# Tables loaded through ScalarE's queue, attention spread over the gated MLP, output stores issued by ScalarE

## The chip, the cores and the metric

One core of one Trainium2 chip runs the whole program. The metric is the device time of one execution in microseconds (us). Engines are named as in the profile: PE is TensorE (PEld its weight loads), DVE is VectorE, ACT is ScalarE, POOL is GpSimd, SP is SyncE, which in the kernel before only issues DMAs. Each engine runs its own instructions strictly in the order in which they were written.

## The reference, cut to what matters

```python
B, H, S, D = 4, 8, 768, 64                      # attention with a decaying state, 8 heads
for t in range(S):
    state = gamma * state + outer(k[:, :, t], v[:, :, t])
    y[:, :, t] = scale * einsum('bhd,bhde->bhe', q[:, :, t], state)
x = y.transpose(0, 2, 1, 3).reshape(B, S, H * D)    # 4 x 768 x 512
gate_pre[s] = sum over 5 taps of conv_w[k] * x[s - 4 + k]   # causal, per channel
gate = 1 / (1 + exp(-gate_pre))
out = (gate * (x @ w_val)) @ w_out                  # two 512x512 matrices
```

## The kernel before, in words

The 768 tokens are cut in 6 chunks of 128 and the 4 batch entries are taken in turn, so attention has 24 steps `g` of (batch, chunk). A step loads 1 MB (`att`: q, k, v and k again in the layouts that the matmuls want), scales v by the decay on POOL (`decay`), multiplies q and k on PE (`scores`, into PSUM `sy`), masks the result on DVE (`mask`, into `u`), and adds on PE the part from the scores (`y_scores`), the update of the running state (`state`, in PSUM `z_ps`) and the part from the state (`y_state`, which reads copies `snap` that ACT makes). DVE then multiplies the sum by a table and writes it into `x` (`evac`). These matmuls are 64x64 in f32; each runs as two passes, so a step of a middle chunk is 128 weight loads and 128 matmuls in the profile: 32 for `scores`, 32 for `y_scores`, 16 for each of two `state`s, 32 for `y_state`.

The gated MLP works on six groups `n` of 512 rows (one chunk of all four batch entries), in four tiles `m` of 128 channels. `val_tile` is 12 matmuls of 128x512 (high and low parts of `x` against high and low parts of `w_val`), `out_tile` 12 more against `w_out`; 24 tiles of each, 576 matmuls. The gate of a tile is a convolution of five taps: the first on ACT, the others on DVE (a few on PE, `pe_tap`), then a sigmoid on ACT. `split`, `gated`, `round_gv` and `rest_gv` make the high and low parts on ACT, DVE and POOL. `store` copies an output tile out of PSUM on ACT; `send` issues its DMA on SP's queue. The two weight matrices and the taps arrive as 64-bit floats; `convert` turns each of eight weight pieces into f32 with five DVE instructions, and some on ACT and POOL.

The order of all engines comes from a planner. Every instruction is a `Step` with a due time, an engine, a cost and what it reads and writes; `plan` orders steps by due time and lets the engine that is free first take the ready step that is earliest due. Due times come from constants: the first six attention steps (`EARLY`) start at `EARLY_AT` and follow each other by `EARLY_STEP`; the other eighteen start at `LATE_AT` and follow by `LATE_STEP`; the MLP tiles start at `MLP_AT` and follow by `MLP_STEP`; `W_AT` holds the due times of the weight conversions. The costs and due times only order the instructions; nothing waits for a clock.

In the first six steps two PSUM tiles for `sy` are in use; the first `val_tile` needs the place of one of them, so it comes after all of them. From the seventh step on the scores of the next step are issued behind `y_state` of this one, in the same `sy`, which is why `y_scores` of a step waits for `evac` of the step before.

Five `att` buffers (`LB`) and four weight buffers (`WB`) set when loads can start. The DMAs of both queues share eight completion semaphores in turn, so a DMA waits for the eighth DMA before it.

In the change and the prediction "the sixth x" is the `evac` of g = 5, "the eleventh x" that of g = 10.

Of the kernel before, what the change touches and what calls it, by code (L numbers as in the profile page):

```python
# [16 lines left out]
P = 128  # L17
# [23 lines left out]
class Step:  # L41
    def __init__(self, due, engine, cost, reads, writes, fn, args):
        self.due, self.engine, self.cost, self.fn, self.args = due, engine, cost, fn, args
        self.reads, self.writes = reads, writes
        self.waits, self.then = set(), []
        self.next = []
        self.after = []
        self.ready = 0.0
        self.words = 0
        self.other = None  # L50


def plan(steps):

    steps = sorted(steps, key=lambda s: s.due)
    writer, readers, rings, users = {}, {}, {}, {}
    for i, s in enumerate(steps):
        s.index = i
        for k in s.writes:
            if isinstance(k, Slot) and k not in users:  # L60
# [24 lines left out]
    for ring in rings.values():  # L85
        for i, (k, s) in enumerate(ring):
            if i >= k.bufs:
                for b in users[ring[i - k.bufs][0]]:
                    wait(s, b)
            if i and s not in ring[i - 1][1].next:  # L90
                s.waits.add(ring[i - 1][1].index)
                ring[i - 1][1].next.append(s)
    clock, free = {}, {}

    def offer(s):
        free.setdefault(s.engine, []).append(s)
        if s.other:
            free.setdefault(s.other[0], []).append(s)

    for s in steps:  # L100
        clock.setdefault(s.engine, 0.0)
        if not s.waits:
            offer(s)
    order, words, paged = [], PAGE - 28, [0.0, 0.0]
    while any(free.values()):
        start, _, e = min(
            (max(clock[e], min(s.ready for s in f)), e, e) for e, f in free.items() if f
        )
        s = min((s for s in free[e] if s.ready <= start), key=lambda s: (s.engine != e, s.index))
        free[s.engine].remove(s)  # L110
        if s.other:
            free[s.other[0]].remove(s)
            if s.engine != e:
                s.engine, s.cost, s.fn = s.other
        order.append(s)
        clock[e] = start + s.cost
        if e == "PE" and s.words:

            left, now = s.words, start
            while left >= words:  # L120
                now += s.cost * words / s.words
                left -= words
                paged.append(now)
                now, words = max(now, paged[-2] + FETCH), PAGE
            words -= left
            clock[e] = max(clock[e], now + s.cost * left / s.words)
        for t in s.next:
            t.ready = max(t.ready, start)
            if t not in s.then:
                t.waits.discard(s.index)  # L130
                if not t.waits:
                    offer(t)
        for t in s.then:
            late = LANDING if e == "DMA" else 0.0 if t.engine == e else LATENCY
            t.ready = max(t.ready, clock[e] + late)
# [8 lines left out]
def tile_retention_gated_mlp(  # L144
# [34 lines left out]
    nc = tc.nc  # L179
# [19 lines left out]
    small_sb = const.tile([P, small.shape[1]], F32, name="small_sb")  # L199
# [20 lines left out]
    def at(due, engine, cost, reads, writes, fn, *args):  # L220
        steps.append(Step(due, engine, cost, list(reads), list(writes), fn, args))
# [12 lines left out]
        nc.sync.dma_start(out=tiles[g][:, part], in_=att[i, :, part])  # L234

    def get(dst, src):
        nc.sync.dma_start(out=dst, in_=src)

    def halves(g, what):

# [267 lines left out]
        outs[n, b, cs.start] = o_sb[:, 0:step]  # L508

    def send(n, b, cs=slice(0, DM)):  # L510
        nc.sync.dma_start(out=out[b, n * P:(n + 1) * P, cs], in_=outs.pop((n, b, cs.start)))


    warm = nc.const_aps.tensor(0.0, (P, 1), F32).bitcast(BF16)[:, 0:1]
# [15 lines left out]


    MM = 0.232
    EARLY_AT = 2.6
    EARLY_STEP = 2.8
    LATE_AT = 28.7
    LATE_STEP = 3.05
    MLP_AT = 31.2
    MLP_STEP = 10.2
    SPLIT_LEAD = 5.4
    CONV_LEAD = 6.1  # L540
    W_AT = (9.3, 15.6, 15.6, 22.7, 32.7, 35.7, 38.7, 41.7)

    loaded = {}

    def load_at(due, g):
        loaded[g] = due
        a = [("att", g % LB, "qk"), ("att", g % LB, "vk")]
        if g == 0:
            at(due, "DMA", 1.4, [], a[0:1], load, g, slice(0, 2))
            at(due, "DMA", 0.2, [], ["small"], get, small_sb, small)  # L550
            at(due, "DMA", 1.4, [], a[1:2], load, g, slice(2, 4))
            at(due, "DMA", 0.1, [], ["cwraw"], get, cw_raw,
               conv_w.bitcast(I32).rearrange("p (n two) -> p n two", two=2))
# [12 lines left out]
        if ahead and g + 1 < NG:  # L566
            scores(g + 1)

    scored, summed = {}, {}

    def attention(g, t, ahead):

# [33 lines left out]
        if b == 0:  # L606
            xbufs[c] = Slot("x", XB)
            last = [xbufs[c - 1]] + [("x", c - 1, i) for i in range(B)] if c else []
            at(t + 3.5, "ACT" if c else "DVE", 0.25, last,
               [xbufs[c]] + [("x", c, i) for i in range(B)], new_x, c)  # L610
        at(t + 5.0, "DVE", 0.62, [y, ("dec", c % 2), xbufs[c]], [("x", c, b)], evac, g)
        if g + LB < NG:
            load_at(t + 3.4, g + LB)
# [83 lines left out]
    at(0, "ACT", 1.5, [], ["table"], first_sigmoid)  # L697
    load_at(0, 0)
    for due, w, n in ((0.1, 1, 0), (0.2, 0, 1), (0.3, 1, 1), (0.4, 0, 2), (0.5, 1, 2), (0.6, 0, 3), (0.7, 1, 3), (0.8, 0, 4)):
        if w or n < LB:  # L700
            (load_w_at if w else load_at)(due, n)
        if due == 0.3:
            at(due, "DMA", 0.2, [], ["eye"], get, eye_sb, eye)
    at(5.05, "PE", 1.0, ["pos", ("att", 0, "vk")], ["sy1"], first_pos)
    at(5.06, "ACT", 0.6, ["sy1"], ["base", ("dec", 0)], base_copy)
    convert(4.0, "cw")
# [16 lines left out]
    order += [(out_tile, NU - 1, m) for m in range(NPAIR)]  # L723
    for p, (what, n, m) in enumerate(order):
        t = MLP_AT + MLP_STEP * p
# [99 lines left out]
```

## Time and profile before

| | |
|---|---|
| median of three runs | 234.3 us (234.22 to 234.41) |
| the profiled execution's own time | 235.24 us |
| its span, first to last instruction | 233.5 us |
| busy PE, DVE, ACT, POOL | 209.3, 140.2, 105.7, 105.7 us |
| mean granted PE clock | 0.954 |

The span is what the views of the profile cover; 1.74 us of the profiled execution lie outside it. The profiled execution took 0.94 us more than the median of the other runs. "Idle before, <-" names what an engine waited for; "issue" is time in which it waited for nothing that the profile shows. A busy PE is one with a matmul in flight, not PE at its peak.

### The profile page before, as it was taken

What the parts mean: (1) busy time and instruction counts of PE and PEld (TensorE: products, weight loads), DVE (VectorE), ACT (ScalarE), POOL (GpSimd) and SP (SyncE); (2) the same over time, 40 slices, a digit from 0 to 9 for tenths busy, and PEclk for the clock granted to TensorE, in tenths of its full rate; (3) what the DMA queues carried; (4) which work ended last, traced back from release to release, by engine and by line L of the source; (5) the groups of instructions that cost most, each with busy time, mean ns of one, the idle gap of its engine ahead of it and who ended that gap; (6) DMA issues with size and microseconds to landing.
All of it is one profiled execution on the core that took longest, in us unless ns stands there. A gap on an engine that the chain in (4) does not pass through costs nothing.

```text
span 233.5 us, 7952 instructions
## 1 busy us (share of the span) xinstructions
PE 209.3 (90%) x3549; PEld 163.5 (70%) x3549; DVE 140.2 (60%) x213; ACT 105.7 (45%) x218; POOL 105.7 (45%) x93
## 2 busy tenths in 40 slices
PE   8276666998799998897998999999999999999994
PEld 3166655766577776675776778888888888888884
DVE  0488678999999998322296636169617861921100
ACT  2363285238855842243544322664376426521322
POOL 0257879677996281116822020582078208220400
PEclk9975697999999999998899999999999999999999
DMA  5999979963565665545250101111111111111122
GB/s 155 381 428 413 380 276 345 414 234 117 181 219 206 243 239 199 206 173 215 65 213 3 48 4 49 45 46 45 48 45 45 45 47 63 59 58 45 45 93 90
DMA packets 8822, 36.32 MB, mean 156 GB/s; under 512 B 1106, under 2 KB 1618, under 8 KB 5844
## 3 DMA queue, kind: packets, MB, share of 16 engines
q1 hardware_dynamic: 8788, 35.82, 41.0%
q8 instruction: 28, 0.46, 0.8%
q14 instruction: 6, 0.05, 0.1%
HBM read 29.52 MB, written 6.29 MB: 153 GB/s over the span
## 4 chain that ended last, share of the span: by engine, by line
PE 61%; DVE 19%; issue 7%; POOL 5%; ACT 3%; DMA 3%; SPq 0%; POOLq 0%; ACTq 0%; DVEq 0%
PE mm L497 27%; PE mm L469 22%; DVE acc L443 9%; PE sy L297 6%; PE sy L259 3%; DMA att<-in_att_dram 3%; PE z_ps L281 3%; DVE x L342 3%; DVE u L269 2%; POOL rest L411 2%; POOL att L249 2%; DVE gate L478 1%; ACT xh L351 1%; DVE rest L415 1%; POOL wvl L430 1%
## 5 line engine op out<-in xcount | busy, mean ns | idle before, releaser
L443 DVE SCALAR_TENSOR_TENSOR acc<-x,cw_sb,acc 128x512 f32<-128x512 f32 x95 | 70.5, 753 | 17.2 <-ACT acc L441 15.1
L489 POOL TENSOR_TENSOR gvl<-gate,gvh 128x512 fp32r<-128x512 f32 x24 | 30.8, 1291 | 44.6 <-ACT gvh L485 34.4
L355 POOL TENSOR_TENSOR xl<-x,xh 128x512 fp32r<-128x512 f32 x24 | 30.5, 1284 | 31.8 <-PE mm L469 28.5
L497 PE MATMUL mm<-woh,gvh 128*128 128x512 f32 (+1 forms) x100 | 39.4, 394 | 0.0
L497 PE MATMUL mm<-wol,gvh 128*128 128x512 f32 (+1 forms) x100 | 39.3, 393 | 0.0
L497 PE MATMUL mm<-woh,gvl 128*128 128x512 f32 (+1 forms) x100 | 39.3, 393 | 0.0
L249 POOL TENSOR_TENSOR att<-att,small_sb 128x512 f32<-128x512 f32 x24 | 25.1, 1044 | 29.1 <-DMA att<-in_att_dram 27.3
L507 ACT COPY o_sb<-mm 128x512 f32<-128x512 f32 (+1 forms) x25 | 14.3, 571 | 37.0 <-PE mm L497 36.9
L269 DVE TENSOR_TENSOR u<-sy,small_sb 128x512 f32<-128x512 f32 x24 | 16.5, 686 | 24.0 <-PE sy L259 24.0
L478 DVE TENSOR_TENSOR gate<-mm,gate 128x512 f32<-128x512 f32 x24 | 16.4, 685 | 22.2 <-PE mm L469 22.2
L469 PE MATMUL mm<-xl,wvh 128*128 128x512 f32 x96 | 28.5, 407 | 0.0
L469 PE MATMUL mm<-xh,wvh 128*128 128x512 f32 x96 | 28.2, 410 | 0.0
L469 PE MATMUL mm<-xh,wvl 128*128 128x512 f32 x96 | 28.1, 404 | 0.0
L485 ACT CAST gvh<-gate 128x512 fp32r<-128x512 f32 x24 | 14.9, 620 | 26.2 <-DVE gate L478 17.6
L297 PEld LDWEIGHTS sy<-u,att 64*64 64x64 f32 x768 | 16.0, 152 | 14.4 <-issue 5.8
L259 PE MATMUL sy<-att 64*64 64x64 f32 x768 | 18.8, 232 | 7.4 <-issue 6.3
L297 PE MATMUL sy<-u,att 64*64 64x64 f32 x768 | 19.1, 243 | 5.9 <-DVE x L342 3.6
L281 PE MATMUL z_ps<-att 64*64 64x64 f32 x704 | 22.1, 240 | 2.3 <-issue 1.0
L292 ACT COPY snap<-z_ps 128x256 f32<-128x256 f32 x44 | 14.5, 371 | 19.0 <-PE z_ps L281 19.0
L281 PEld LDWEIGHTS z_ps<-att 64*64 64x64 f32 x704 | 17.3, 150 | 8.1 <-ACT snap L292 5.2
L259 PEld LDWEIGHTS sy<-att 64*64 64x64 f32 x768 | 15.9, 147 | 9.0 <-issue 7.0
L497 PEld LDWEIGHTS mm<-woh,gvh 128*128 128x128 f32 x100 | 18.9, 189 | 4.2
(46 smaller groups left out, 264.6 us busy)
## 6 DMA issues: line engine op xcount, KB each, us to landing
att<-in_att_dram SPq DMA_DIRECT2D x23, 1024.0 KB, 5.8
out_dram<-o_sb SPq DMA_DIRECT2D x23, 256.0 KB, 2.0
wst<-in_w_dram SPq DMA_DIRECT2D x8, 512.0 KB, 7.2
att<-in_att_dram SPq DMA_DIRECT2D x2, 512.0 KB, 5.5
out_dram<-o_sb SPq DMA_DIRECT2D x2, 128.0 KB, 1.7
small_sb<-in_small_dram SPq DMA_DIRECT2D x1, 68.0 KB, 4.1
eye_sb<-in_eye_dram SPq DMA_DIRECT2D x1, 64.0 KB, 8.5
cw_raw<-in_conv_w_dram SPq DMA_DIRECT2D x1, 20.0 KB, 6.4
```

Of the source, the lines that this page charges most:

```text
L249: nc.gpsimd.tensor_tensor(v, v, vd_sb[:, c, :].unsqueeze(2).broadcast_to([P, 8, HALF]), op=ALU.mult)
L259: nc.tensor.matmul(sy[cols, x, (2 * j + s) * HALF:(2 * j + s + 1) * HALF], lhsT=kT[rows, x, j, s, :], rhs=q[rows, x, j, s, :], start=True, ...
L269: nc.vector.tensor_tensor(us[g], sy[:, :, 0:256].rearrange("p x (a t) -> p x a t", t=HALF), tri_sb.unsqueeze(1).unsqueeze(1).broadcast_to( ...
L281: nc.tensor.matmul(z_ps[cols, x, b, j], lhsT=k[rows, x, j, s, :], rhs=v[rows, x, j, s, :], start=g == 0 and s == 0 and j == 0, stop=True, ...
L297: nc.tensor.matmul(sy_of(g)[cols, h, off:off + HALF], lhsT=lhsT, rhs=rhs, start=start, stop=True, skip_group_check=True,)
L355: nc.gpsimd.tensor_tensor(xl[n, ct], xs[n][:, ct, :, HALO:], xh[n, ct].bitcast(F32), op=ALU.subtract)
L443: nc.vector.scalar_tensor_tensor(acc, x[:, :, k:k + P], cw_sb[:, m, k:k + 1], acc, op0=ALU.mult, op1=ALU.add,)
L469: nc.tensor.matmul(vps[n, m], lhsT=w[:, m, ct * P:(ct + 1) * P], rhs=xx[n, ct].rearrange("p b t -> p (b t)"), start=(i == 0), stop=(i == 3 ...
L478: nc.vector.tensor_tensor(gv, vps.pop((n, m)), gv, op=ALU.mult)
L485: nc.scalar.copy(gvs[n, m][0], gate[n, m])
L489: nc.gpsimd.tensor_tensor(gvl, gate.pop((n, m)), gvh.bitcast(F32), op=ALU.subtract)
L497: nc.tensor.matmul(ops[n, b, cs.start][:, 0:cs.stop - cs.start], lhsT=gg[:, b * P:(b + 1) * P], rhs=w[:, ct, cs], start=(i == 0), stop=(i ...
```

## The change

It does five things.

1. `small`, `pos`, `conv_w` and `eye` are loaded through ACT's queue, ahead of ACT's first instruction, and the two halves of the first `att` follow each other on SP's queue. `first_pos` no longer waits for the second half of `att`.
2. On DVE the first mask is moved ahead of most of the conversion of the taps.
3. `send` issues the output DMA on ACT, a few instructions behind the copy that it sends, instead of on SP.
4. The due times change: late attention steps follow each other by 6.0 instead of 3.05, MLP tiles by 3.6 instead of 10.2, and a `val_tile` is due no earlier than its `x` is whole.
5. The planner's own cost of a fetch of PE instructions changes.

```diff
-PAGE, FETCH = 128, 4.0
+PAGE, FETCH, CROWDED = 128, 3.4, 5.0
...
     def get(dst, src):
-        nc.sync.dma_start(out=dst, in_=src)
+        nc.scalar.dma_start(out=dst, in_=src)
...
     def send(n, b, cs=slice(0, DM)):
-        nc.sync.dma_start(out=out[b, n * P:(n + 1) * P, cs], in_=outs.pop((n, b, cs.start)))
+        nc.scalar.dma_start(out=out[b, n * P:(n + 1) * P, cs], in_=outs.pop((n, b, cs.start)))
...
-    LATE_STEP = 3.05
+    LATE_STEP = 6.0
...
-    MLP_STEP = 10.2
+    MLP_STEP = 3.6
...
         if g == 0:
-            at(due, "DMA", 1.4, [], a[0:1], load, g, slice(0, 2))
-            at(due, "DMA", 0.2, [], ["small"], get, small_sb, small)
-            at(due, "DMA", 1.4, [], a[1:2], load, g, slice(2, 4))
-            at(due, "DMA", 0.1, [], ["cwraw"], get, cw_raw,
+            at(due, "DMA", 3.2, [], a[0:1], load, g, slice(0, 2))
+            at(due, "DMA", 1.6, [], a[1:2], load, g, slice(2, 4))
+            at(due, "ACT", 0.4, [], ["small"], get, small_sb, small)
+            at(due, "ACT", 0.4, [], ["pos"], get, pos_sb, pos)
+            at(due, "ACT", 0.4, [], ["cwraw"], get, cw_raw,
...
-            at(due, "DMA", 0.1, [], ["pos"], get, pos_sb, pos)
+            at(due, "ACT", 0.4, [], ["eye"], get, eye_sb, eye)
...
-            at(t0 + 12 * MM / cols + 0.2, "DMA", 0.1, [o], [], send, n, b, cs)
+            at(t0 + 12 * MM / cols + 0.2, "ACT", 0.07, [o], [], send, n, b, cs)
...
+        if what is val_tile:
+            t = max(t, whole[n] + max(SPLIT_LEAD, CONV_LEAD))
```

What this does to the order is shown at three places. The first is DVE at the start of the program; `cw_raw` is the raw taps, `wst` a raw weight piece, `sy` and `u` the scores and the masked scores. Before:

```order
L386 TENSOR_SCALAR acc<-cw_raw 128x20
L392 SCALAR_TENSOR_TENSOR top<-cw_raw,acc 128x20
L398 TENSOR_SCALAR acc<-top 128x20
L402 SCALAR_TENSOR_TENSOR rest<-cw_raw,acc 128x20
L415 SCALAR_TENSOR_TENSOR cw_sb<-acc,rest 128x20
L386 TENSOR_SCALAR acc<-wst 128x512
L269 TENSOR_TENSOR u<-sy,small_sb 128x512
```

Now, on the same engine from the same place:

```order
L388 TENSOR_SCALAR acc<-cw_raw 128x20
L394 SCALAR_TENSOR_TENSOR top<-cw_raw,acc 128x20
L271 TENSOR_TENSOR u<-sy,small_sb 128x512
L400 TENSOR_SCALAR acc<-top 128x20
L404 SCALAR_TENSOR_TENSOR rest<-cw_raw,acc 128x20
L388 TENSOR_SCALAR acc<-wst 128x512
L394 SCALAR_TENSOR_TENSOR top<-wst,acc 128x512
```

The mask of the first step stands behind two small instructions of the conversion instead of six.

The second place is PE from the first `val_tile` (g = 6) to `y_scores` of g = 7; `mm` is a tile of the MLP, `sy<-u,att` is `y_scores`, `sy<-att,snap` is `y_state`, `sy<-att` is `scores`. Before:

```order
L469 MATMUL mm<-xh,wvh 128x512 x4
L281 MATMUL z_ps<-att 64x64 x8
L297 MATMUL sy<-att,snap 64x64 x16
L259 MATMUL sy<-att 64x64 x16
L469 MATMUL mm<-xh,wvl 128x512 x4
L469 MATMUL mm<-xl,wvh 128x512 x4
L469 MATMUL mm<-xh,wvh 128x512 x2
L297 MATMUL sy<-u,att 64x64 x16
```

Now:

```order
L471 MATMUL mm<-xh,wvh 128x512 x4
L471 MATMUL mm<-xh,wvl 128x512
L283 MATMUL z_ps<-att 64x64 x8
L299 MATMUL sy<-att,snap 64x64 x16
L261 MATMUL sy<-att 64x64 x16
L471 MATMUL mm<-xh,wvl 128x512 x3
L471 MATMUL mm<-xl,wvh 128x512 x4
L471 MATMUL mm<-xh,wvh 128x512 x4
L471 MATMUL mm<-xh,wvl 128x512 x4
L471 MATMUL mm<-xl,wvh 128x512 x2
L299 MATMUL sy<-u,att 64x64 x16
```

The step holds 22 matmuls of the MLP instead of 14.

The third place is the middle of the program, SP's queue before, where stores stand between loads:

```order
L234 DMA att<-in_att_dram 128x2048 x6
L511 DMA out_dram<-o_sb 128x512
L234 DMA att<-in_att_dram 128x2048 x2
L511 DMA out_dram<-o_sb 128x512
L234 DMA att<-in_att_dram 128x2048 x2
L511 DMA out_dram<-o_sb 128x512
```

and ACT now, where the first two stores stand among copies of the state, taps and sigmoids:

```order
L294 COPY snap<-z_ps 128x256 x2
L509 COPY o_sb<-mm 128x512
L461 ACTIVATE gate<-acc 128x512
L513 DMA out_dram<-o_sb 128x512
L443 ACTIVATE acc<-x,cw_sb 128x512
L461 ACTIVATE gate<-acc 128x512
L487 CAST gvh<-gate 128x512
L509 COPY o_sb<-mm 128x512
L513 DMA out_dram<-o_sb 128x512
```

SP's queue now ends in loads alone, thirteen of them in a row; all 25 stores stand on ACT.

More of the change, by code (lines that the diff above doesn't have):

```diff
@@ L47, in __init__ @@
         self.after = []
+        self.lag = 0.0
         self.ready = 0.0
@@ L123, in plan @@
                 paged.append(now)
-                now, words = max(now, paged[-2] + FETCH), PAGE
+                slow = clock.get("DMA", 0.0) > now
+                now, words = max(now, paged[-2] + (CROWDED if slow else FETCH)), PAGE
             words -= left
@@ L134, in plan @@
             late = LANDING if e == "DMA" else 0.0 if t.engine == e else LATENCY
-            t.ready = max(t.ready, clock[e] + late)
+            t.ready = max(t.ready, clock[e] + late + s.lag)
             t.waits.discard(s.index)
@@ L532, in tile_retention_gated_mlp @@
     MM = 0.232
-    EARLY_AT = 2.6
-    EARLY_STEP = 2.8
-    LATE_AT = 28.7
-    LATE_STEP = 3.05
-    MLP_AT = 31.2
-    MLP_STEP = 10.2
-    SPLIT_LEAD = 5.4
-    CONV_LEAD = 6.1
-    W_AT = (9.3, 15.6, 15.6, 22.7, 32.7, 35.7, 38.7, 41.7)
+    EARLY_AT = 3.46
+    EARLY_STEP = 2.26
+    LATE_AT = 29.71
+    LATE_STEP = 6.0
+    MLP_AT = 31.96
+    MLP_STEP = 3.6
+    SPLIT_LEAD = 5.44
+    CONV_LEAD = 6.16
+    W_AT = (9.3, 13.0, 15.6, 22.7, 36.8, 32.1, 37.6, 38.1)
     loaded = {}
@@ L548, in load_at @@
         if g == 0:
-            at(due, "DMA", 1.4, [], a[0:1], load, g, slice(0, 2))
-            at(due, "DMA", 0.2, [], ["small"], get, small_sb, small)
-            at(due, "DMA", 1.4, [], a[1:2], load, g, slice(2, 4))
-            at(due, "DMA", 0.1, [], ["cwraw"], get, cw_raw,
+            at(due, "DMA", 3.2, [], a[0:1], load, g, slice(0, 2))
[3 more added lines that the diff above has]
+            at(due, "ACT", 0.4, [], ["cwraw"], get, cw_raw,
                conv_w.bitcast(I32).rearrange("p (n two) -> p n two", two=2))
-            at(due, "DMA", 0.1, [], ["pos"], get, pos_sb, pos)
+            at(due, "ACT", 0.4, [], ["eye"], get, eye_sb, eye)
+            for s in steps[-4:]:
+                s.lag = 5.0
         else:
@@ L567, in block_b @@
             scores(g + 1)
-    scored, summed = {}, {}
+    scored, summed, whole = {}, {}, {}
     def attention(g, t, ahead):
@@ L610, in attention @@
                [xbufs[c]] + [("x", c, i) for i in range(B)], new_x, c)
+        whole[c] = t + 5.1
         at(t + 5.0, "DVE", 0.62, [y, ("dec", c % 2), xbufs[c]], [("x", c, b)], evac, g)
@@ L692, in out_tile @@
             at(t0 + 12 * MM / cols + 0.1, "ACT", 0.6 / cols, [bank], [o], store, n, b, cs)
-            at(t0 + 12 * MM / cols + 0.2, "DMA", 0.1, [o], [], send, n, b, cs)
+            at(t0 + 12 * MM / cols + 0.2, "ACT", 0.07, [o], [], send, n, b, cs)
     for i in range(WARM):
         at(0, "PE", 0.43, [], [Slot("acc", 2) if i < 2 else "sy1"], warm_up, i)
-    at(0, "ACT", 1.5, [], ["table"], first_sigmoid)
     load_at(0, 0)
+    at(0.05, "ACT", 1.5, [], ["table"], first_sigmoid)
     for due, w, n in ((0.1, 1, 0), (0.2, 0, 1), (0.3, 1, 1), (0.4, 0, 2), (0.5, 1, 2), (0.6, 0, 3), (0.7, 1, 3), (0.8, 0, 4)):
@@ L701, in tile_retention_gated_mlp @@
             (load_w_at if w else load_at)(due, n)
-        if due == 0.3:
-            at(due, "DMA", 0.2, [], ["eye"], get, eye_sb, eye)
-    at(5.05, "PE", 1.0, ["pos", ("att", 0, "vk")], ["sy1"], first_pos)
+    at(5.05, "PE", 1.0, ["pos"], ["sy1"], first_pos)
     at(5.06, "ACT", 0.6, ["sy1"], ["base", ("dec", 0)], base_copy)
-    convert(4.0, "cw")
+    convert(9.0, "cw")
     for m in range(NPAIR):
@@ L723, in tile_retention_gated_mlp @@
     order += [(out_tile, NU - 1, m) for m in range(NPAIR)]
+    t = MLP_AT - MLP_STEP
     for p, (what, n, m) in enumerate(order):
-        t = MLP_AT + MLP_STEP * p
+        t += MLP_STEP
+        if what is val_tile:
+            t = max(t, whole[n] + max(SPLIT_LEAD, CONV_LEAD))
         if what is val_tile:
```

## The prediction

> **What bounds the kernel now.** I read the page first, then busy time in stretches of my choice, then the chain that ended last, then the timeline of the places that the change touches. From the page:
>
> ```profile
> span 233.5 us, 7952 instructions
> PE 209.3 (90%) x3549; PEld 163.5 (70%) x3549; DVE 140.2 (60%) x213; ACT 105.7 (45%) x218; POOL 105.7 (45%) x93
> ```
>
> The 90% is an average over four stages. I cut the span where they change: 38.70 is the start of `y_scores` of g = 6, just ahead of the first MLP tile, 67.21 the end of `y_state` of g = 10, 139.36 the start of the stretch without attention matmuls. Columns are the stretch, its length, busy time of PE, PEld, DVE, ACT, POOL with instruction counts, granted PE clock, DMA share and GB/s:
>
> ```profile
> 0.00:38.70 38.70, 24.59 (x746) 18.84 (x750) 24.82 (x43) 18.91 (x45) 22.14 (x24) 0.82 0.90 343
> 38.70:67.21 28.51, 26.08 (x676) 20.19 (x674) 27.51 (x43) 16.21 (x35) 23.64 (x21) 0.95 0.66 246
> 67.21:139.36 72.15, 67.63 (x1749) 50.95 (x1741) 46.17 (x69) 30.72 (x70) 29.49 (x26) 0.98 0.43 152
> 139.36:233.50 94.14, 90.96 (x416) 73.55 (x408) 41.71 (x59) 39.82 (x68) 30.43 (x24) 1.00 0.14 54
> ```
>
> The first stage is bound by none of the engines (PE is busy 24.59 of 38.70 us, DVE 24.82), the second by DVE (27.51 of 28.51), the last by PE. The third looks like PE, but busy is not peak, so I count its work. The chain shows a tile of 12 MLP matmuls at full rate, and the last copy:
>
> ```profile
> 140.70 2.80 PE mm L469 x12
> 230.40 0.37 ACT o_sb L507
> ```
>
> That is 0.2333 us for a matmul. Then one attention step, packed without a gap, from `scores` done to the next `y_scores`, of a middle chunk and of the last chunk:
>
> ```profile
> 117.32:123.44 6.12, 6.12 (x144) 4.71 (x143) 5.94 (x10) 2.24 (x6) 1.05 (x1) 1.00 0.44 179
> 127.78:132.45 4.67, 4.66 (x122) 3.54 (x122) 4.18 (x6) 1.23 (x3) 0.00 (x0) 1.00 0.16 58
> ```
>
> The order puts 15 and 10 MLP matmuls into them, 3.50 and 2.33 us, so attention costs PE 2.62 us a step, and 2.34 in the last chunk. How much of the MLP is done by 67.21 (the `val_tile` line alone; `out_tile` has none there):
>
> ```profile
> 38.70:67.21 28.51, 15.24 (x53) 0.95 0.66 246
> ```
>
> So 576 - 53 = 523 matmuls and 13 steps (9 of 2.62, 4 of 2.34: 32.9 us) are left at 67.21: 67.2 + 523 x 0.2333 + 32.9 = 222.1, where the copy starts at 230.4. The stages after 67.21 lose 8.3 us in waits. These I find in the timeline:
>
> ```profile
> 92.72 0.69 PE L297 MATMUL sy<-u,att 64*64 64x64 f32 x32 [0.67 <-DVE x L342]
> 96.69 0.34 PE L259 MATMUL sy<-att 64*64 64x64 f32 x7 [0.90 <-issue]
> 102.18 0.56 PE L259 MATMUL sy<-att 64*64 64x64 f32 x19 [0.26 <-issue]
> 108.93 0.68 PE L259 MATMUL sy<-att 64*64 64x64 f32 x29 [1.51 <-issue]
> 110.00:115.00 5.00, 5.00 (x112) 3.66 (x113) 1.55 (x3) 2.15 (x5) 3.82 (x4) 0.69 0.32 134
> 127.79 0.69 PE L297 MATMUL sy<-u,att 64*64 64x64 f32 x32 [0.75 <-DVE x L342]
> ```
>
> They make 4.1 us, and the clock of 0.69 for 5 us behind the longest of them another 1.6; the rest is small change.
>
> **Early part.** Before, the first mask stands behind the conversion of the taps, which waits for them to land:
>
> ```profile
> 1.17 0.42 SPq L237 DMA_DIRECT2D small_sb<-in_small_dram  x1
> 1.64 0.42 SPq L234 DMA_DIRECT2D att<-in_att_dram  x1
> 5.21 0.69 PE L259 MATMUL sy<-att 64*64 64x64 f32 x32
> 8.43 1.04 POOL L249 TENSOR_TENSOR att<-att,small_sb 128x512 f32<-128x512 f32 x1 [7.99 <-DMA att<-in_att_dram]
> 8.62 0.18 DVE L386 TENSOR_SCALAR acc<-cw_raw 128x20 int32<-128x20 int32 x1 [7.69 <-DMA cw_raw<-in_conv_w_dram]
> 10.53 0.68 DVE L269 TENSOR_TENSOR u<-sy,small_sb 128x512 f32<-128x512 f32 x1
> 11.31 1.13 PE L297 MATMUL sy<-u,att 64*64 64x64 f32 x32 [1.81 <-issue]
> ```
>
> Scores are there at 5.90. With the taps and `small` on another queue the mask can run by 7, and `y_scores` waits for v, which POOL has scaled at 9.47: a gain of 11.31 - 9.6 = 1.7 us. The second half of `att` is issued 0.47 us earlier (1.17 instead of 1.64), so up to 2.2. Is that kept until the MLP? PE then waits at regular places:
>
> ```profile
> 18.41 0.80 PE L259 MATMUL sy<-att 64*64 64x64 f32 x18 [1.57 <-issue]
> ...
> 38.21 0.81 PE L297 MATMUL sy<-att,snap 64*64 64x64 f32 x20 [1.37 <-issue]
> 18.40:24.51 6.11, 4.05 (x127) 3.71 (x127) 4.35 (x7) 2.24 (x4) 4.51 (x5) 0.50 1.02 418
> q8 instruction: 28, 0.46, 0.8%
> ```
>
> There are five such waits from 18.41 to 38.21, each about 128 matmuls behind the last (127 in the stretch shown). The q8 row has 28 packets for 7952 instructions, 284 each, so 128 matmuls with their 128 loads are about one packet: PE waits for its own instructions, 4.95 us from one to the next, while loads fill the DMA engines (share 1.02). The change keeps the number of matmuls ahead of the first MLP tile, so this clock moves with its first tick, which is set by when the first step is through. Bounds: 0 if the loads set the pace, 2.2 if all of it is carried. I take 2.0, near the upper end, because the wait at 18.41 is for instructions and not for a load. The sixth `x` (39.17 before) then is at 37.2.
>
> Here a rule speaks against me: the Trainium skill, page "Runtime: NRT & Kernel Launch", section "Instruction fetch mechanics", has instructions come in blocks of 256 and calls the crossing "mostly hidden". The trace agrees on the block (127 matmuls and as many loads) and not on the hiding (1.57 us at 18.41); by the rule the waits would have another cause, and the 2.0 would rest on the loads alone, near 0.
>
> **DVE part.** From the sixth to the eleventh `x` DVE has 45 instructions before, 13 of them taps and 3 gates, and is busy 29.20 of 29.73 us:
>
> ```profile
> 39.17:68.90 29.73, 27.30 (x695) 21.16 (x688) 29.20 (x45) 17.26 (x37) 24.86 (x22) 0.96 0.64 232
> 39.16:68.89 29.73, 9.68 (x13) 0.96 0.64 232
> 40.49 0.71 DVE acc L398
> 73.65 0.68 DVE gate L478
> 74.33 0.60 DVE u L269
> 86.03 5.36 DVE L443 SCALAR_TENSOR_TENSOR acc<-x,cw_sb,acc 128x512 f32<-128x512 f32 x7
> ```
>
> The new order has between the same two `x` 21 taps, 6 gates, one conversion instruction more and one mask fewer: 8 x 0.77 + 3 x 0.68 + 0.71 - 0.60 = 8.3 us, less 0.4 because a gate behind other work adds 0.60 rather than 0.68 and DVE's idle 0.5 is filled in part. 29.7 + 7.9 = 37.6. PE needs less there: 84 MLP matmuls (19.6) and five steps (13.1), 32.7. So DVE stays the bound of this part, and the eleventh `x` comes at 37.2 + 37.6 = 74.8. Ahead of it DVE runs a gate, 7 taps, a gate and a tap (7.3 us) while PE runs three quarters of a step and 14 matmuls (2.0 + 3.3), so `y_state` of g = 10 ends 2.0 earlier, at 72.8. This is 5.6 us later than before, but with 84 matmuls done instead of 53, 7.2 us of work.
>
> **Late part.** Left are 576 - 84 = 492 matmuls, 114.8 us, and 32.9 of attention: 72.8 + 147.7 = 220.5. From the copy to the span's end stay 233.5 - 230.4 = 3.1. Which waits stay? Each step now has 17 to 22 MLP matmuls instead of 5 to 13. Packets are passed slower: 147 matmuls in some 7 us, 6.1 a packet, where the waits above came at 5.5 and 6.75 us. These came when two or three loads were issued in one go behind a store:
>
> ```profile
> 89.87 5.97 SPq L234 DMA_DIRECT2D att<-in_att_dram  x2
> 101.93 13.60 SPq L234 DMA_DIRECT2D att<-in_att_dram  x3
> out_dram<-o_sb SPq DMA_DIRECT2D x23, 256.0 KB, 2.0
> 230.80 0.33 SPq L511 DMA_DIRECT2D out_dram<-o_sb  x1
> ```
>
> With the stores on ACT loads are let go one by one. Against that DVE runs 3 to 7 taps between two masks; counted over the new order it is later than PE by 0.5, 0.3 and 0.4 us at three steps, 1.2 in all, and PE waits for `snap` a little more than before. I take 2.0 us of waits, between 0 and the 8.3 of before. A store costs ACT the issue, 0.33 us on SP; no row has it on ACT, so between 0 and the 2.0 of its landing, and I take 0.4, as near to SP's own. ACT is busy 30.72 of 72.15 us there, and twelve times 0.4 is covered by the 2 to 8 matmuls that PE runs between `y_scores` and `y_state`. If the matmuls were not there, `snap` would be late and PE with it. The DMA semaphore that a store waits for belongs to a load three or more steps back.
>
> Span: 72.8 + 147.7 + 3.1 + 2.0 = 225.6. The profiled execution spent 1.74 outside its span and was 0.94 above the median: 226.4.
>
> **The rivals.** (a) The loads set the early pace: DMA share is 1.02 while the first steps run. Only the 0.47 of the earlier issue is left: 226.4 + 1.5 = 227.9. For it speaks the share; against it that PE's wait at 18.41 is not put down to a load. The Trainium skill, "DMA: Bandwidth & Descriptors", section "Issuing engines are not separate DMA queues", agrees: a second issuing engine saves only issue time. (b) The waits of the late part are not of too many instructions in too short a time, and spreading does not touch them: 8.3 instead of 2.0, 232.7. For it speaks that steps of 10 to 15 matmuls were passed without a wait up to 90 us; against it the place of the three waits, behind bursts of loads. This is what the skill's rule on instruction blocks would lead to. (c) Slower: a store holds ACT until it has landed, 2.0 us, and `snap` stands behind it. Less a cover of 0.9 (four matmuls) that is 1.1 at each of the 12 stores that lie among attention: 226.4 + 13 = 239.6. It decides from 0.9 + 7.9 / 12 = 1.6 us a store on. Against it: the next copy has another buffer, and only the second next must wait for the landing. (d) a and b together: 234.2, no change.
>
> **How the numbers follow.** 0.62 for the forecast (its own range 223.0, with no waits, all 2.2 early and 1.2 less in the DVE part, to 229.0, with 1.4 less early and 1.2 more waits), 0.14 for a, 0.14 for b, 0.06 for c, 0.04 for d. About 0.2% is what a measurement of this kernel can tell. Faster holds the forecast, a and b: 0.90; same d: 0.04; slower c: 0.06. From 223.0 to 232.8 all but c, d and the edges are held.
>
> **What would show it.** Right: the first `y_scores` near 9.5; the sixth `x` near 37, the eleventh near 75 with DVE busy between; no stretch of the late part with a clock under 0.9; about 208 matmuls left without attention at the end, in 2.80 us tiles. Wrong: issue waits in the late part once a step; DVE idle between the sixth and the eleventh `x` (its taps waiting for ACT); `y_state` waiting for `snap` behind a store.

## The result, and the profile after

The changed kernel takes 228.88 us (median of four runs, 228.31 to 229.09) where the kernel before takes 234.36 on the same chip (234.22 to 235.38): a ratio of 0.975, 95% interval 0.972 to 0.979. The profiled execution took 228.31 us, 226.3 of them in the span.

From the page of the changed kernel, the span, the busy times, the granted PE clock in 40 slices and the shares of the chain that ended last:

```profile
span 226.3 us, 7941 instructions
PE 208.8 (92%) x3551; PEld 162.8 (72%) x3551; DVE 140.0 (62%) x212; ACT 106.7 (47%) x218; POOL 105.9 (47%) x93
PEclk9857559999999999999999999999999999999999
PE 80%; DVE 10%; issue 4%; DMA 2%; POOL 1%; ACT 1%; ACTq 0%; POOLq 0%
```

PE's work is nearly the same (208.8 us busy against 209.3), so 6.7 of the 7.2 us that the span lost are idle time that went. The clock row says where: behind the sixth slice there is no digit below 9, where the kernel before had a 7 in the seventh slice and an 8 in the 19th and the 20th:

```profile
PEclk9975697999999999998899999999999999999999
```

The same in stretches, cut at the sixth `x`, the eleventh `x`, the end of `y_state` of g = 10 and the start of the stretch without attention (columns as before: stretch, length, busy time of PE, PEld, DVE, ACT, POOL, clock, DMA share, GB/s):

```profile
38.84:76.65 37.81, 34.50 (x726) 26.25 (x718) 36.95 (x57) 23.03 (x46) 27.79 (x24) 1.00 0.51 180
...
74.98:168.35 93.37, 93.37 (x1874) 72.59 (x1865) 56.47 (x84) 45.10 (x94) 38.34 (x32) 1.00 0.38 135
168.35:219.90 51.55, 51.55 (x222) 41.52 (x223) 22.51 (x32) 19.28 (x32) 15.28 (x12) 1.00 0.13 51
```

The first row is DVE's part, 36.95 of 37.81 us busy. In the other two PE is busy in every microsecond: no wait shows behind 75 us. The 8.3 us of waits and slow clock of the late part are gone altogether.

The first part kept almost nothing of its gain. From the timeline, the first `y_scores`, PE's waits for instructions and the sixth `x` at 38.84:

```profile
9.91 1.13 PE L299 MATMUL sy<-u,att 64*64 64x64 f32 x32 [1.87 <-issue]
22.67 0.21 PE L261 MATMUL sy<-att 64*64 64x64 f32 x1 [2.22 <-issue]
27.97 0.36 PE L283 MATMUL z_ps<-att 64*64 64x64 f32 x1 [0.83 <-issue]
38.20 0.52 PE L299 MATMUL sy<-att,snap 64*64 64x64 f32 x20 [1.79 <-issue]
38.84 0.69 DVE L344 TENSOR_TENSOR x<-sy,dec 128x512 f32<-128x512 f32 x1 [0.55 <-PE sy L299]
```

`y_scores` starts 1.40 earlier than before. The waits for instructions end 1.85 earlier (22.67 against 24.52) and 1.73 earlier (27.97 against 29.70), and the last ends where it ended before (38.20 against 38.21). The sixth `x` has 0.33 of the gain left.

### The profile page after: what moved, and what is told of

The parts are those of the page before. It is cut to its first block, busy times and chain, and to the rows that moved or that the text cites. A ratio compares the mean times of both kernels' runs of the same rounds, so it can differ in the third digit from the quotient of the medians.

```text
span 226.3 us, 7941 instructions
## 1 busy us (share of the span) xinstructions
PE 208.8 (92%) x3551; PEld 162.8 (72%) x3551; DVE 140.0 (62%) x212; ACT 106.7 (47%) x218; POOL 105.9 (47%) x93
## 4 chain that ended last, share of the span: by engine, by line
PE 80%; DVE 10%; issue 4%; DMA 2%; POOL 1%; ACT 1%; ACTq 0%; POOLq 0%
PE mm L499 28%; PE mm L471 27%; PE sy L299 10%; PE z_ps L283 5%; PE sy L261 5%; PE sy L521 2%; DVE acc L445 2%; DMA out_dram<-o_sb 2%; DVE acc L400 1%; DVE x L344 1%; DVE rest L417 1%; DVE top L394 1%; POOL rest L413 1%; DVE u L271 1%; PE acc L454 1%
## 5 line engine op out<-in xcount | busy, mean ns | idle before, releaser
L471 PE MATMUL mm<-xl,wvh 128*128 128x512 f32 x96 | 27.8, 402 | 0.0
L471 PE MATMUL mm<-xh,wvl 128*128 128x512 f32 x96 | 27.4, 400 | 0.0
L283 PEld LDWEIGHTS z_ps<-att 64*64 64x64 f32 x704 | 17.2, 151 | 10.2 <-ACT snap L294 6.2
L461 ACT ACTIVATE gate<-acc 128x512 f32<-128x512 f32 x24 | 14.3, 596 | 18.7 <-POOL gvl L491 10.8
L344 DVE TENSOR_TENSOR x<-sy,dec 128x512 f32<-128x512 f32 x20 | 13.8, 689 | 14.8 <-PE sy L261 14.2
L294 ACT COPY snap<-z_ps 128x256 f32<-128x256 f32 x44 | 15.2, 372 | 15.7 <-PE z_ps L283 15.3
L499 PEld LDWEIGHTS mm<-wol,gvh 128*128 128x128 f32 x100 | 18.8, 188 | 4.1
```

Of the source, the lines that this page charges most:

```text
L283: nc.tensor.matmul(z_ps[cols, x, b, j], lhsT=k[rows, x, j, s, :], rhs=v[rows, x, j, s, :], start=g == 0 and s == 0 and j == 0, stop=True, ...
L294: nc.scalar.copy(sn, z_ps[:, :, b])
L344: nc.vector.tensor_tensor(xs[c][:, :, b, HALO:].rearrange("p (h j) t -> p h j t", h=2), sy_of(g)[:, :, 256:512].rearrange("p h (j t) -> p ...
L471: nc.tensor.matmul(vps[n, m], lhsT=w[:, m, ct * P:(ct + 1) * P], rhs=xx[n, ct].rearrange("p b t -> p (b t)"), start=(i == 0), stop=(i == 3 ...
L499: nc.tensor.matmul(ops[n, b, cs.start][:, 0:cs.stop - cs.start], lhsT=gg[:, b * P:(b + 1) * P], rhs=w[:, ct, cs], start=(i == 0), stop=(i ...
```

## The experiments

The theory (A): the even spread of attention emptied the late part, because PE then uses up its instructions more slowly than they come; the queues gave next to nothing; and the early gain was eaten by PE's waits for instructions. Against it stood, in turn, that the queues brought it (B), that the loads alone set the early pace, and that DVE's order held the sixth `x`. The runs came from several chips, where the kernel before took 235.1 to 235.7 us, so ratios to it are given.

**Stores back on SP (e1).** The changed kernel with

```diff
-        nc.scalar.dma_start(out=out[b, n * P:(n + 1) * P, cs], ...)
+        nc.sync.dma_start(out=out[b, n * P:(n + 1) * P, cs], ...)
```

> The changed kernel with its order on PE, DVE and POOL untouched; only the output stores are issued on SP's queue again, where they stand between the loads. Theory A (the even spread packs the late part, the stores' engine matters little): 228.9 us within 0.5, no instruction waits on PE from 80 to 165 us. Theory B (the three waits of before came from loads that stood behind stores and were let go in bursts): waits of about 0.9 us return at several packet ends, 231 to 234 us. If a store on ACT is dear, this is up to 1 us faster than the changed kernel.

Measured: 227.55 us, ratio 0.967 (0.960 to 0.975), span 225.9, no wait in the late part. The store on ACT takes away no wait of the late part. Nor is a cost of it shown: the interval overlaps that of the changed kernel (0.972 to 0.979).

**Tables back on SP (e2).** `get` on `nc.sync` again, all else as changed.

> The changed kernel with its order on PE, DVE and POOL untouched; only the four tables are loaded on SP's queue again, small first, ahead of and between the halves of the first load as the order has them. Theory A (early time is paced by instructions and weight conversions, and is lost again by the sixth x): first y_scores later by 0.5 to 1.5 us, the sixth x within 0.4 of 38.84, total 228.9 within 0.7. Theory B (the early gain is carried to the end): total later by as much as the first y_scores, 229.5 to 230.5 us.

Measured: 228.34 us, ratio 0.971 (0.965 to 0.977), span 226.8. From its timeline:

```profile
6.05 0.18 DVE L388 TENSOR_SCALAR acc<-cw_raw 128x20 int32<-128x20 int32 x1 [5.12 <-DMA cw_raw<-in_conv_w_dram]
...
8.77 1.04 POOL L251 TENSOR_TENSOR att<-att,small_sb 128x512 f32<-128x512 f32 x1 [8.33 <-DMA att<-in_att_dram]
9.87 0.69 PE L299 MATMUL sy<-u,att 64*64 64x64 f32 x32 [2.29 <-POOL att L251]
...
39.80 0.69 DVE L344 TENSOR_TENSOR x<-sy,dec 128x512 f32<-128x512 f32 x1 [0.33 <-PE sy L299]
```

and the same two rows of the changed kernel:

```profile
6.52 1.04 POOL L251 TENSOR_TENSOR att<-att,small_sb 128x512 f32<-128x512 f32 x1 [6.08 <-DMA att<-in_att_dram]
8.82 0.18 DVE L388 TENSOR_SCALAR acc<-cw_raw 128x20 int32<-128x20 int32 x1 [7.89 <-DMA cw_raw<-in_conv_w_dram]
```

On SP the taps land in time and v is late. In the changed kernel it is the other way round. The first `y_scores` starts at 9.87 or 9.91: for it, the queue only chose which of the two holds it, and both theories, which had it 0.5 us later or more, missed that. The sixth `x` comes 0.96 later than in the changed kernel, more than the 0.4 that A allowed, behind a second wait for instructions that ends 6.07 us after the first instead of 5.30. The time is within what A gave.

**The kernel before with stores on ACT (e3).** The same edit as e1, the other way round, on the kernel before.

> The kernel before with its order on PE, DVE and POOL untouched; only the output stores are issued on ACT. Theory A (the waits of before at 96, 102 and 108 us come from too many attention matmuls in too short a time): they stay, 234.3 us within 0.5. Theory B (they come from loads behind stores): they go, and with them 2.7 us and the slow clock of 1.6, 230 us. If a store on ACT holds up the copies of the state, slower than 234.3.

Measured: 235.64 us, ratio 1.001 (0.998 to 1.005). Its timeline has the waits of the late part still:

```profile
97.88 0.34 PE L259 MATMUL sy<-att 64*64 64x64 f32 x7 [0.62 <-issue]
103.64 0.56 PE L259 MATMUL sy<-att 64*64 64x64 f32 x19 [0.53 <-issue]
109.84 0.68 PE L259 MATMUL sy<-att 64*64 64x64 f32 x29 [0.97 <-issue]
115.31 0.28 PE L297 MATMUL sy<-att,snap 64*64 64x64 f32 x3 [0.63 <-issue]
```

2.75 us in four waits, 2.67 in three before, though SP's queue there holds no store between the loads: that loads stand behind stores was not their cause. The Trainium skill, page "DMA: Bandwidth & Descriptors", section "Issuing engines are not separate DMA queues", says that a second issuing engine saves issue time alone; the times of e1, e2 and e3 agree, as none differs from its kernel beyond the intervals.

**The spread alone (e4).** The kernel before with

```diff
-    LATE_STEP = 3.05
+    LATE_STEP = 6.0
...
-    MLP_STEP = 10.2
+    MLP_STEP = 3.6
...
+            t = max(t, whole[n] + max(SPLIT_LEAD, CONV_LEAD))
```

> The kernel before with the due times of the late attention steps and of the MLP alone changed (6.0 and 3.6, a val_tile due no earlier than its x is whole); tables and stores stay on SP, the planner's fetch cost and the early due times stay. Theory A (the spread is the change that pays): a late part without waits, 228.5 to 230.5 us, at most 1 us from the changed kernel. Theory B (stores between loads make the waits): 231 to 234 us, with instruction waits in the late part.

Measured: 231.88 us, ratio 0.985 (0.979 to 0.992), span 230.1. PE in a stretch of the late part:

```profile
80.00:165.00 85.00, 85.00 (x1668) 66.00 (x1672) 50.56 (x75) 39.84 (x85) 33.77 (x29) 1.00 0.41 145
```

and, from the timeline, its one large wait behind the sixth `x`:

```profile
60.63 2.07 PE L452 MATMUL acc<-x,diag 128*128 128x512 f32 x2 [4.12 <-ACT acc L441]
```

The late part is free of waits by the spread alone, as A had it; the time is above the 228.5 to 230.5 that A gave. The span is 3.8 longer than in the changed kernel, where no such wait of 4.12 stands. In e4 the tap on ACT that PE waits for starts at 59.89, behind the step of a weight conversion on ACT that had waited 2.11 for DVE's `rest`. The change also moved the early due times (`EARLY_AT`, `EARLY_STEP`) and those of the conversions (`W_AT`), which e4 leaves as they were. That `W_AT` is what is missing here is argued, not shown.

**The changed kernel again (e5), and with the old density (e6).** In e6:

```diff
-    LATE_AT = 29.71
-    LATE_STEP = 6.0
-    MLP_AT = 31.96
-    MLP_STEP = 3.6
+    LATE_AT = 28.7
+    LATE_STEP = 3.05
+    MLP_AT = 31.2
+    MLP_STEP = 10.2
...
-            t = max(t, whole[n] + max(SPLIT_LEAD, CONV_LEAD))
+            t = max(t, 0.0)
```

> The changed kernel itself, as the yardstick for the other runs on this chip. Both theories: 227 to 229 us, span 226 to 227.5, the sixth x near 38.8 and no wait on PE after 45 us.

> The changed kernel with the four numbers of the attention spread put back to those of before (28.7, 3.05, 31.2, 10.2) and the whole-product clause taken out; queues, masks and the other constants stay. Theory A (the even spread is what emptied the late part of PE's waits): PE waits for instructions and for x again between 80 and 130 us, 3 to 8 us of idle in all, and the time is 231 to 235. Theory B (the gain came from the queues and from the order of the first part): the waits stay away and the time is within 1 us of the changed kernel.

Measured: e5 228.46 us, ratio 0.973 (0.969 to 0.977), span 225.9, sixth `x` at 38.68, no wait on PE behind 67 us (four between 42 and 67, for DVE or ACT); e6 238.11 us, ratio 1.015 (1.010 to 1.019), span 236.0. The spread is worth 9.7 us here, more than A gave (231 to 235 us in all); without it the kernel is slower than the one before. PE's waits for instructions in e6, from the timeline:

```profile
99.59 0.33 PE L261 MATMUL sy<-att 64*64 64x64 f32 x4 [1.37 <-issue]
105.34 0.46 PE L261 MATMUL sy<-att 64*64 64x64 f32 x15 [0.48 <-issue]
111.19 0.62 PE L261 MATMUL sy<-att 64*64 64x64 f32 x26 [0.82 <-issue]
117.15 0.27 PE L299 MATMUL sy<-att,snap 64*64 64x64 f32 x2 [0.90 <-issue]
```

and the stretches from each to the next:

```profile
99.59:105.34 5.75, 5.27 (x128) 3.95 (x127) 1.89 (x3) 2.08 (x7) 1.04 (x1) 1.00 0.40 162
105.34:111.19 5.85, 5.03 (x127) 3.74 (x128) 1.29 (x2) 1.85 (x4) 1.04 (x1) 1.00 0.67 227
111.19:117.15 5.96, 5.06 (x128) 3.79 (x128) 1.98 (x3) 2.85 (x6) 4.06 (x4) 1.00 0.49 179
```

These seven rows show the mechanism. A packet is 128 matmuls with their 128 weight loads. PE is done with one in 5.0 to 5.3 us, the next is there 5.75 to 5.96 after the last, and PE waits for the rest. Queue q8, which carries the instructions, bears it out: read to 0.1 us, its packets move at 97.3, 102.4, 108.8 and 114.8, each 2.3 to 2.9 us ahead of the end of one of these waits. Loads have a part in it: from the end of a wait to the next packet pass 2.8, 3.5 and 3.6 us while the DMA engines are busy 0.79 to 0.86 of the time, and 1.05 us behind 117.15, where they are idle. Spread evenly, PE cannot run so far ahead (a stretch of the changed kernel):

```profile
80.00:130.00 50.00, 50.00 (x1009) 38.92 (x1011) 30.28 (x45) 24.84 (x54) 22.92 (x20) 1.00 0.51 181
```

128 of 1009 matmuls in 50 us take 6.3 us, longer than the 5.96, and nothing is waited for. Of the 9.7 us, PE's waits that the timeline shows behind 75 us make 6.2; the rest lies ahead of that and in small gaps, and was not taken apart. Nor was it settled why e6 falls behind the kernel before.

The Trainium skill, "Runtime: NRT & Kernel Launch", section "Instruction fetch mechanics", calls the crossing of a block of instructions "mostly hidden". At 6.3 us a block the trace agrees; at 5.0 to 5.3 it does not, with 0.48 to 1.37 us at each crossing.

**Loads of g = 5 and later left out (e7).**

```diff
+        if g >= LB:
+            tiles[g] = tiles[g - LB]
+            return
```

> The changed kernel, in which att tiles of g = 5 and later are not loaded, the tiles of g - 5 being read again: it leaves out these loads and so computes other numbers. Theory A (PE's waits for instructions at 22.67, 27.97 and 38.20 are long because the loads fill the DMA engines at that time): the waits at 27.97 and 38.20, of 0.83 and 1.79 us, shrink below 0.5 each, the sixth x comes at 36 to 37.5 instead of 38.84, and the time falls by 1 to 2 us. Theory B (the waits are a matter of how fast PE's instructions are used up, whatever the DMA engines do): waits as before within 0.3 us, the sixth x within 0.4 of 38.84, and the time within 0.5 us of the changed kernel.

Measured: 227.28 us, ratio 0.967 (0.964 to 0.970), span 225.3. Its waits for instructions and its sixth `x`:

```profile
22.93 0.21 PE L264 MATMUL sy<-att 64*64 64x64 f32 x1 [1.87 <-issue]
27.26 0.36 PE L286 MATMUL z_ps<-att 64*64 64x64 f32 x1 [0.37 <-issue]
...
38.16 0.68 DVE L347 TENSOR_TENSOR x<-sy,dec 128x512 f32<-128x512 f32 x1
```

The second wait is 4.33 us behind the first, where it is 5.30 and 5.35 behind it in the changed kernel and in e5. So the loads do slow the packets. The third wait is gone, but it is not there in e5 either, so this is not shown to come from the loads. The sixth `x` comes only 0.5 to 0.7 earlier than in e5 and the changed kernel, and not 1.3 or more. A is right on the second wait and too large in the price, because DVE holds `x` as well. In the changed kernel `x` of g = 2 and of g = 3 on DVE, and the step ahead of the latter, are

```profile
24.51 0.68 DVE L344 TENSOR_TENSOR x<-sy,base 128x512 f32<-128x512 f32 x1
...
29.29 0.69 DVE L417 SCALAR_TENSOR_TENSOR rest<-acc,rest 128x512 f32<-128x512 f32 x1 [1.45 <-POOL rest L413]
29.90 0.68 DVE L344 TENSOR_TENSOR x<-sy,base 128x512 f32<-128x512 f32 x1
```

and the same two `x` before

```profile
26.24 0.68 DVE L342 TENSOR_TENSOR x<-sy,base 128x512 f32<-128x512 f32 x1
30.34 0.69 DVE L342 TENSOR_TENSOR x<-sy,base 128x512 f32<-128x512 f32 x1 [0.18 <-PE sy L297]
```

That is 5.39 us against 4.10. It is 5.38 or 5.39 in e1, e2, e5, e7, e9 and e11 too, whether the packet comes 4.33 us behind the one before (e7) or 6.32 (e9). So DVE's new order sets this stretch, and of the 1.73 us by which `x` of g = 2 is earlier it takes 1.29. The early gain was eaten by two chains, and not by PE's waits alone as A has it. In e5 and e7 DVE also comes to the sixth `x` itself without a wait for PE:

```profile
38.68 0.68 DVE L344 TENSOR_TENSOR x<-sy,dec 128x512 f32<-128x512 f32 x1
```

**First mask ahead of the taps, the plan made anew (e8), and by one move in the finished order (e9).** In e8:

```diff
-                s.lag = 5.0
+                s.lag = 7.5 if "cwraw" in s.writes else 5.0
```

> The changed kernel with the conversion of the conv weights behind the first mask on DVE (a lag of 7.5 in place of 5.0 for that step), so that the first mask waits for the first product alone and not for the conv weights' transfer, which landed at 7.9. Theory A (the first products are then bound by v and the start of the chain moves): first y_scores at 7.5 to 8.7 instead of 9.91, but the next PE waits for instructions take most of it back, so that the sixth x comes 0 to 0.5 earlier and the time falls by 0 to 0.5 us. Theory B (what is gained at the start is carried to the sixth x): the sixth x 1.2 to 2 earlier, the time 1 to 2 us shorter.

Measured: 232.28 us, ratio 0.988 (0.983 to 0.992): slower than the changed kernel, which neither theory had. `y_scores` starts at 7.89 and the sixth `x` comes at 37.78, 1.06 earlier. But the planner, given that one number, wrote another order for what follows: one tap moved from PE to DVE, and the stretch from the sixth to the eleventh `x` takes 42.28 us instead of 37.81. It tested two things at once. (The 7.9 in its expectation is the length of DVE's wait; the taps landed near 8.7.) e9 has only this move, on DVE:

```diff
+L271 TENSOR_TENSOR u<-sy,small_sb 128x512
 L388 TENSOR_SCALAR acc<-cw_raw 128x20
 L394 SCALAR_TENSOR_TENSOR top<-cw_raw,acc 128x20
-L271 TENSOR_TENSOR u<-sy,small_sb 128x512
```

> The changed kernel with one move in the finished order of DVE: the first mask stands ahead of the two steps that open the conversion of the conv weights, so that it no longer waits for their transfer; every other instruction of every engine stays in its place. Theory A (the sixth x is held by two chains at once, PE's waits for instructions and the order of DVE, so that a start 2 us earlier is mostly eaten by the first of them): first y_scores near 7.9 instead of 9.5 to 9.9, the sixth x 0.3 to 1.0 earlier than 38.7 to 38.8, and the time 0.3 to 1.0 us shorter. Theory B (the start is carried through): the sixth x 1.6 to 2.0 earlier and the time as much shorter. If the time rises by over 1 us, as in the run in which the plan as a whole was made anew, the early mask itself does harm and both fall.

Measured: 227.88 us, ratio 0.970 (0.965 to 0.974), span 225.0. From its timeline:

```profile
8.18 0.69 PE L299 MATMUL sy<-u,att 64*64 64x64 f32 x32
...
19.24 0.69 PE L261 MATMUL sy<-att 64*64 64x64 f32 x30 [0.91 <-DMA att<-in_att_dram]
21.32 0.21 PE L261 MATMUL sy<-att 64*64 64x64 f32 x1 [1.39 <-issue]
23.19 0.73 PE L261 MATMUL sy<-att 64*64 64x64 f32 x32 [1.14 <-DMA att<-in_att_dram]
27.64 0.37 PE L283 MATMUL z_ps<-att 64*64 64x64 f32 x1 [0.92 <-issue]
37.17 0.52 PE L299 MATMUL sy<-att,snap 64*64 64x64 f32 x20 [1.08 <-issue]
37.80 0.69 DVE L344 TENSOR_TENSOR x<-sy,dec 128x512 f32<-128x512 f32 x1
```

Against the changed kernel the start is 1.73 earlier, the first wait ends 1.35 earlier, the second 0.33 and the third 1.03; the sixth `x` comes 1.04 earlier and the span is 1.3 shorter (0.9 against e5). So a start can be carried, but not whole: PE now waits for loads of `att`, 0.91 and 1.14 us, which it did not in the changed kernel, and the packet at 27.64 came 6.32 us behind the one at 21.32, a microsecond more than there. In the time the gain is not shown: the interval overlaps that of e5.

**Conversion's last step behind `x` of g = 3 (e10).** This is the wait of 1.45 us for POOL that was shown under e7, with `x` of g = 3 queued behind it. One move on DVE:

```diff
+L344 TENSOR_TENSOR x<-sy_97,base 128x4x128
 L417 SCALAR_TENSOR_TENSOR rest<-acc,rest 128x512
-L344 TENSOR_TENSOR x<-sy_97,base 128x4x128
```

> The changed kernel with one move in the finished order of DVE: the last step of the conversion of the fourth weight tile, which waits 1.45 us for POOL at 29.3, stands behind x of g = 3 instead of ahead of it. Theory A (that wait holds x of g = 3 and with it the sixth x): x of g = 3 at 29.0 to 29.7 instead of 29.90 to 30.16, the sixth x 0.3 to 1.0 earlier, the time 0.3 to 1.0 us shorter. Theory B (PE's waits for instructions hold the sixth x whatever DVE does): x of g = 3 moves, the sixth x stays within 0.2 of 38.7 to 38.8 and the time within 0.3.

Measured: 228.45 us, ratio 0.973 (0.969 to 0.977), span 227.0.

```profile
22.19 0.21 PE L261 MATMUL sy<-att 64*64 64x64 f32 x1 [2.10 <-issue]
28.53 0.36 PE L283 MATMUL z_ps<-att 64*64 64x64 f32 x1 [1.86 <-issue]
29.50 0.69 DVE L344 TENSOR_TENSOR x<-sy,base 128x512 f32<-128x512 f32 x1 [2.23 <-PE sy L299]
39.38 0.69 DVE L344 TENSOR_TENSOR x<-sy,dec 128x512 f32<-128x512 f32 x1
```

POOL no longer holds the `x`, PE does: the packet came 6.34 us behind the one before. `x` of g = 3 is 0.4 earlier, the sixth is 0.54 later. Neither theory has that number. PE releases this `x` in e10 only 0.4 us earlier than DVE comes to it in the changed kernel, so to take away DVE's wait alone is no lever.

**Taps k = 3 and 4 of the first gates left out (e11).**

```diff
+    order = [s for s in plan(steps) if not (s.fn is tap and s.args[0] == 0 and s.args[2] >= 3)]
```

> The changed kernel without taps k = 3 and k = 4 of the four gates of the first chunk (it leaves out that part of the convolution): 8 steps of 0.76 us fall out of DVE's order, 3 of them ahead of the sixth x and 5 between the sixth x and the eleventh; all else stays in its place. Theory A (DVE's own work sets the pace from the sixth x to the eleventh): the stretch is shorter by as much as PE had idle there, 2 to 3.3 us of 37.8, after which PE is busy all through; the time falls by 2 to 3.5 us. Theory B (PE's waits or its clock set the pace there): the stretch stays within 0.7 of 37.8 and the time within 0.7 us.

Measured: 226.92 us, ratio 0.965 (0.958 to 0.971), span 225.8. The stretch from the sixth `x` (40.73) to the eleventh (76.36) takes 35.63 us, 2.2 less: DVE set the pace there, and with the taps gone PE does, busy 35.41 of the 35.63. But the sixth `x` came 1.9 later than in the changed kernel, behind this:

```profile
39.75 0.81 PE L299 MATMUL sy<-att,snap 64*64 64x64 f32 x20 [2.34 <-issue]
```

The two cancel but for 0.3 us of the eleventh `x`, and the span is that of e5. Of the 2 to 3.5 us that A gave for the time, the median has 1.5 to 2.0, with an interval that overlaps e5's (0.969 to 0.977): the shorter stretch is shown, its gain at the end is not.

**Mask swapped and stores on SP (e12).** The edits of e9 and e1 together.

> The version that the runs so far point to: the changed kernel with the first mask ahead of the conv weights' conversion in DVE's order, and with the output stores issued by SP again. Theory A (the store's issue on ScalarE is worth nothing to the time and costs at most a little, and the early mask is worth about 1 us at the sixth x): span 224.5 to 226, time 226.3 to 228, ratio to the kernel before 0.962 to 0.972, late part without waits on PE. Theory B (stores on SP get in the loads' way there): waits on PE return between 80 and 165 us, and the span is above 226.5.

Measured: 227.16 us, ratio 0.968 (0.963 to 0.972), span 225.5, no wait in the late part, sixth `x` at 38.45. Its interval and that of e5 (0.969 to 0.977) overlap: that it beats the changed kernel is not shown.

## Why the prediction came out as it did

226.4 was predicted and 228.88 measured, in the range. The forecast had the mechanism of the DVE part and of the late part, where the spread all but frees PE of waits, and not that of the early part. That the sum is this near is luck in part: the 1.64 us that were lost early and the 2.0 us of waits that did not come cancel. Term by term:

| term | predicted | measured | difference |
|---|---|---|---|
| sixth `x` | 37.2 | 38.84 | +1.64 |
| sixth to eleventh `x` | 37.6 | 37.81 | +0.21 |
| `y_state` of g = 10 ends ahead of the eleventh `x` by | 2.0 | 1.67 | +0.33 |
| from there to the end of the late part, without waits | 147.7 | 147.86 | +0.16 |
| waits in it | 2.0 | 0 | -2.0 |
| tail | 3.1 | 3.46 | +0.36 |
| outside the span | 1.74 | 2.01 | +0.27 |
| median less profiled execution | -0.94 | +0.57 | +1.51 |

- **The DVE part and the late part were right**: two counts from the new order, 37.6 and 147.7, are off by 0.21 and 0.16. "About 208" matmuls left without attention was a miscount, though no term of the sum: from 168.35 on the trace has 88 of `val_tile` and 144 of `out_tile` (24 of them halves counted as 12), 232.
- **The step that failed is the early gain**, "I take 2.0, near the upper end, because the wait at 18.41 is for instructions and not for a load". It was 0.33 in the profiled execution and 0.49 in e5. The first tick did move, by 1.40, and `x` of g = 2 with it, by 1.73. That "this clock moves with its first tick" fails in two ways. The sum has no term for DVE ahead of the sixth `x`, though the change gives it a new order there; that order, with its wait for POOL, takes 1.29 of the gain between `x` of g = 2 and of g = 3 (5.39 us instead of 4.10, in e7 and e9 alike). And the time from one packet to the next is no constant. It is 4.33 us in e7, 5.30 in the changed kernel, 6.32 in e9 and 6.34 in e10, for the same 128 matmuls; even the five waits of before, 4.95 apart in the mean, were 6.11, 5.18, 3.71 and 4.80 apart. Rival (a), the loads, has part of it: without them the packet comes sooner (e7), and with an earlier start PE runs into the landing of `att` itself (e9). Its time, 227.9, was nearer than the forecast for the early part: 1.5 less gain, where 1.64 were lost.
- **What stays open there** is the PE clock: from the first `y_scores` to the sixth `x` it was granted at 0.65, before at 0.75, and PE was busy 21.01 us with 724 matmuls, before 18.81 with 719. No run takes this apart from the waits.
- **The first tick** came near the 9.5 of the forecast by luck. v, taken as ready at 9.47, was scaled by 7.56; the mask, put at 7, ran at 9.13, behind taps that landed late on ACT's queue.
- **The waits** were put at 2.0 for DVE's taps between two masks and for `snap` behind stores. None came: DVE, behind its busy part, is ahead of PE and waits for it, as here in the changed kernel:

```profile
97.41 0.69 DVE L344 TENSOR_TENSOR x<-sy,dec 128x512 f32<-128x512 f32 x1 [4.45 <-PE sy L261]
```

- **The burst of loads behind stores**, given for the late waits, was wrong in the stores: e3 takes them out of the loads' way and the waits stay. The loads themselves do delay PE's packets, as queue q8 shows in e6. It cost the sum nothing, as the spread removes them anyhow (e4, e5 against e6).
- **The store on ACT** was charged nothing on the path, and e1, e3 and e12 show no cost beyond the intervals.
- **The largest of the other errors is the scale**: the profiled execution of before happened to lie 0.94 above its median, and that of after 0.57 below. Without this last row the sum is off by 0.97.

Rival (b), late waits untouched, falls with e4 and e6. So does (d), which needs (b). Rival (c), a store that holds ACT, falls with e1 and e3.

## What to carry to other kernels

Count how fast PE passes blocks of instructions, stretch by stretch: where small matmuls crowd and loads are under way, PE may wait for instructions while every engine and queue that it depends on looks free, and mixing large matmuls in removes the wait without removing any work. A time saved ahead of such waits is carried only as far as the next of them, or as the next engine whose order has no slack: follow it through each engine. When a planner sets the order, change the finished order by one move to test one thing; a changed due time or lag may rewrite stages far behind it.

## What was not expected of the hardware

- The next 128 matmuls and 128 weight loads came 4.3 to 6.3 us behind the last ones in the first part, and 7.3 in e11 (from about 32.4, counted back over 128 matmuls, to 39.75), in kernels whose order on PE is the same (the changed kernel, e5, e7, e9, e10, e11). What varies is the time until the packet moves. In the first part of these runs, q8's packet moved 1.05 to 1.2 us behind the end of a wait where the DMA engines were busy up to 0.67 of that time, and 1.35 to 4.9 us behind it where they were busy 0.93 or more; PE went on 2.4 to 2.6 us behind the packet, once 3.3 (e7). Each is read from one execution of a kernel.
- A 20 KB transfer that was third on ACT's queue landed 7.0 us behind its issue while the loads filled the DMA engines, and 3.9 us behind it on SP's queue (e2), with one half of the first load ahead of it: a queue of its own did not make a small transfer early.
